# A nine-way router: "not computed" as a choice of its own, one summing instruction per tile for the slots

## The chip, the cores and the metric

The kernel runs on one core of a Trainium2 chip. The metric is the device time of one execution in microseconds; the time given is the median of the timed runs. Views of the trace come from one further, profiled execution. The engines are PE (TensorE: matmuls, with PEld for its weight loads), DVE (VectorE), ACT (ScalarE), POOL (GpSimd) and SP (SyncE, which issues most of the DMAs).

## What is computed

Three layers follow one another: an attention with a threshold per row, a dense two-matrix layer with a smooth activation, and a mixture of eight experts. 4 batches of 576 rows give 2304 tokens of width 512. The change lies in the third layer's router:

```python
skip_score = x @ w_skip
do_compute = skip_score > 0
out = x.copy()
xc = x[do_compute]
logits = xc @ w_gate                       # 8 experts
e_idx = np.argmax(logits, axis=1)
probs = softmax(logits)
gate_w = probs[np.arange(len(xc)), e_idx]
for e in range(8):
    mask = e_idx == e
    h = np.maximum(xc[mask] @ w1[e], 0.0)
    y[mask] = gate_w[mask, None] * (h @ w2[e])
out[do_compute] = xc + y
```

## The kernel before

The attention is worked off in units of one head and 128 rows (two heads for the last 64 rows of a batch), the dense layer in ten blocks of 128 or 256 tokens. Both run interleaved, since the blocks need only the rows that are finished. A planner (`Plan`, `P.op`) gets every operation with its engine, a nominal duration, what it follows, its buffers and a due time; it simulates the engines and so fixes one order of issue per engine. The order depends on the nominal durations, not on what the operation's code contains. At run time each engine works off its queue in that order, and an instruction that waits holds up all behind it on its engine.

The router (`class Route`) takes the dense layer's blocks in eleven groups: one of a single tile of 128 tokens, seven of two tiles, three of a single tile at the end. For each group the planner issues:

- `rsq` (ACT), for the last three groups `rtp` (PE) and `rsq`: `begin` takes the small tile `sm`, which has a few columns per tile of the group, and the squares of the row are summed into `ss`.
- `rinv` (DVE, L279): `pow2_scale` (L28 to L31, four instructions) makes a power of two `inv` and its inverse `rin` for each tile.
- `rhi`, `rlo`, `rtr`, `rlog`: the rows are split into two halves of 16 bits, transposed by DMA, and multiplied with the nine columns of weights (eight experts and skip) into PSUM, `d["l"]`. The last three groups use PE for the transposition and multiply in fp32.
- `rpick` (DVE, L312 to L340): the maximum, a weight 8 to 1 for each expert that reaches it, the largest of these, and the one-hot row `c` of eight columns, multiplied with `cmp` (skip score above 0).
- `rrank` (PE, L342): a matmul with a triangle and one with ones and `csum` count, for each token, how many earlier tokens chose each expert.
- `rslot` (DVE, L351 to L361): the count plus the expert's offset, times `c`, summed: the row of the table `tbl` into which the token goes. The offset begins at -BIG, so a token that isn't computed gets a row beyond the table, which the write leaves out. Then `csum` takes in `c`.
- `rexp` (ACT, L366), `rgate` (DVE, L369 to L377): the gate, and the table entry `meta` of three numbers: token, gate times `rin`, and `inv`.
- `rsc` (POOL, L381): an indirect DMA writes the entries into `tbl`.

For the last two groups one-hot matrices (L276) are made from the slots, with which PE takes the first two experts' rows straight from the tiles. Behind the router lie the counts, the load of the table and the experts.

The constants are made at `rconst` (L206), between two pieces of the attention. The first DVE instructions there fill `ones16` and `csum`; POOL makes the triangle, the weights `w8` (L212), the offsets `offs` (L213) and the token numbers `tok`.

```python
    def rinv(s, ts):
        d = s.st[ts]
        for i in range(len(ts)):
            pow2_scale(s.nc, None, d["ss"][:, i], d["inv"][:, i], d["rin"][:, i], 195)
```

Of the kernel before, what the change touches and what calls it, by code (L numbers as in the profile page):

```python
# [188 lines left out]
class Route:  # L189
    def __init__(s, nc, cst, dram, w_skip, w_gate):  # L190
        s.nc = nc
        s.w_skip, s.w_gate = w_skip, w_gate
        s.tri = cst.tile([128, 128], F16, name="tri")
        s.ones16 = cst.tile([128, 128], F16, name="ones16")
        s.w8 = cst.tile([128, NE], F32, name="w8")
        s.offs = cst.tile([128, NE], F32, name="offs")
        s.wg = cst.tile([128, 4, NE + 1], F32, name="wg")
        s.wg16 = cst.tile([128, 2, 4, NE + 1], F16, name="wg16")
        s.wsc = cst.tile([128, 4], F32, name="wsc")
        s.csum = cst.tile([128, NE], F16, name="csum")  # L200
        s.tok = cst.tile([128, NT // 128], I32, name="tok")
        s.tbl = dram.tile([NE * NT, 3], I32, name="tbl")
        s.x2d = dram.tile([NT, DM], F32, name="x2d")
        s.st = {}

    def consts(s):  # L206
        nc = s.nc
        nc.vector.memset(s.ones16, 1.0)
        nc.vector.memset(s.csum, 0.0)
        nc.gpsimd.affine_select(out=s.tri, in_=s.ones16, pattern=[[1, 128]], compare_op=ALU.is_gt, fill=0.0, base=0,  # L210
                                channel_multiplier=-1)
        nc.gpsimd.iota(s.w8, pattern=[[-1, NE]], base=NE, channel_multiplier=0, allow_small_or_imprecise_dtypes=True)  # L212
        nc.gpsimd.iota(s.offs, pattern=[[NT, NE]], base=-BIG, channel_multiplier=0,  # L213
                       allow_small_or_imprecise_dtypes=True)
        nc.gpsimd.iota(s.tok, pattern=[[128, NT // 128]], base=0, channel_multiplier=1)
        big = s.junk.bitcast(I32)[:, 0:NT * NE // 128]
        nc.gpsimd.iota(big, pattern=[[0, NT * NE // 128]], base=BIG, channel_multiplier=0)
        nc.sync.dma_start(out=s.wg[:, :, 0:NE], in_=s.w_gate.rearrange("(k p) e -> p k e", p=128))
        nc.sync.dma_start(out=s.wg[:, :, NE:NE + 1], in_=s.w_skip.rearrange("(k p) -> p k", p=128)[:, :, None])
        for i in range(3):  # L220
            nc.sync.dma_start(out=s.tbl.rearrange("(i a b) c -> i a (b c)", i=3, a=128)[i], in_=big)
# [11 lines left out]

    def begin(s, ts, xs):
        sm = s.wk.tile([128, 114], F32, tag="sm", bufs=4, name="sm")
        v, o = {}, 0
        for k, w in (("ss", 1), ("inv", 1), ("kap", 1), ("mx", 1), ("nb", 1), ("cmp", 1), ("top", 1), ("sl", 1),
                     ("sum", 1), ("rin", 1), ("va", 8), ("vb", 8), ("vc", 8)):
# [73 lines left out]
    def pick(s, ts, plain=False):  # L312

        nc, d, n = s.nc, s.st[ts], len(ts)
        c = s.wk.tile([128, 2, NE], F16, tag="c", bufs=4, name="c")[:, 0:n]
        d["c"] = c
        l = d["l"][:, :, 0:NE]
        w8 = s.w8[:, None, :].to_broadcast([128, n, NE])

        def wide(x):  # L320
            return x.to_broadcast([128, n, NE])
        nc.vector.tensor_reduce(out=d["mx"], in_=l, axis=AX.X, op=ALU.max)
        if n == 1:
            nc.vector.scalar_tensor_tensor(out=d["va"][:, 0], in0=l[:, 0], scalar=d["mx"][:, 0], in1=s.w8, op0=ALU.is_ge, op1=ALU.mult)
        else:
            nc.vector.tensor_tensor(out=d["va"], in0=l, in1=wide(d["mx"]), op=ALU.is_ge)
            nc.vector.tensor_tensor(out=d["va"], in0=d["va"], in1=w8, op=ALU.mult)
        nc.vector.tensor_scalar(out=d["cmp"], in0=d["l"][:, :, NE:NE + 1], scalar1=0.0, scalar2=None, op0=ALU.is_gt)
        nc.vector.tensor_reduce(out=d["top"], in_=d["va"], axis=AX.X, op=ALU.max)
        if n == 1:  # L330
            nc.vector.scalar_tensor_tensor(out=c[:, 0], in0=s.w8, scalar=d["top"][:, 0], in1=d["cmp"][:, 0].to_broadcast([128, NE]),
                                           op0=ALU.is_equal, op1=ALU.mult)
        else:
            nc.vector.tensor_tensor(out=d["vb"], in0=w8, in1=wide(d["top"]), op=ALU.is_equal)
            nc.vector.tensor_tensor(out=c, in0=d["vb"], in1=wide(d["cmp"]), op=ALU.mult)
        if plain:
            nc.vector.memset(d["kap"], 1.0)
        else:
            nc.vector.tensor_scalar(out=d["kap"], in0=d["rin"], scalar1=s.wsc[:, 2:3], scalar2=None, op0=ALU.mult)
        nc.vector.scalar_tensor_tensor(out=d["nb"], in0=d["mx"], scalar=-1.0, in1=d["kap"], op0=ALU.mult, op1=ALU.mult)  # L340

    def rank(s, ts):  # L342
        d = s.st[ts]
        for i in range(len(ts)):
            r = d["r"][:, i, 0:NE]
# [22 lines left out]

    def rgate(s, ts):  # L369
        nc, d, n = s.nc, s.st[ts], len(ts)  # L370
        m = s.wk.tile([128, 2, 3], I32, tag="meta", bufs=4, name="meta")
        d["m"] = m
        nc.vector.tensor_scalar(out=d["sum"], in0=d["sum"], scalar1=1e-9, scalar2=None, op0=ALU.add)
        nc.gpsimd.tensor_copy(out=m[:, 0:n, 0], in_=s.tok[:, ts[0]:ts[0] + n])
        nc.vector.reciprocal(out=d["sum"], in_=d["sum"])
        nc.vector.tensor_copy(out=m[:, 0:n, 2:3].bitcast(F32), in_=d["inv"])
        nc.vector.tensor_tensor(out=m[:, 0:n, 1:2].bitcast(F32), in0=d["sum"], in1=d["rin"], op=ALU.mult)  # L377

    def scatter(s, ts, i):
        d = s.st[ts]  # L380
# [338 lines left out]
def body(ctx, tc, q, k, v, tau, w_in, w_out, w_skip, w_gate, w1, w2, out):  # L719
# [968 lines left out]
```

## Time and profile before

| | us |
|---|---|
| median of three timed runs | 984.99 |
| lowest and highest of them | 982.43, 986.34 |
| the profiled execution | 978.3 |
| its span, from the first to the last instruction | 976.3 |
| PE busy | 813.4 (83%) |
| DVE busy | 708.7 (73%) |
| ACT busy | 612.2 (63%) |
| POOL busy | 497.7 (51%) |

The page's slices and the table of stretches are read first: they show where each engine is busy. The lists of waits say which engine ended an idle time. The groups by line and shape give the mean duration of one instruction, which includes the time in which it was held after its start. The timeline gives single instructions in their order, with the idle time in front of each.

### The profile page before, as it was taken

The page shows a single profiled execution, that of the slowest core. Times are in us where ns is not written, and L with a number is a line of the kernel's source. Part 1 is how long each engine was busy: PE and PEld are TensorE (multiplying, and loading weights), DVE is VectorE, ACT ScalarE, POOL GpSimd, SP SyncE. Part 2 cuts the span into 40 slices and gives each one's busy share as a digit, 9 for nine tenths or more (in the row PEclk, how much of TensorE's full clock was granted, in tenths as well). Part 3 has the DMA queues.
Part 4 walks back from the last instruction along what each step waited for, and adds up shares of the span by engine and source line. Part 5 has one row for each costly group of instructions (what it writes and reads, how often), then busy time and mean ns, then how long its engine had stood idle before and what let it go on. Part 6 is the DMA issues. An engine that isn't in the chain of part 4 may idle for free. (4 is left out here: it accounts for less than half of the span.)

```text
span 976.3 us, 19887 instructions
## 1 busy us (share of the span) xinstructions
PE 813.4 (83%) x7340; PEld 588.1 (60%) x7340; DVE 708.7 (73%) x1433; ACT 612.2 (63%) x1003; POOL 497.7 (51%) x454
## 2 busy tenths in 40 slices
PE   6476875778889899857998988979989887999994
PEld 3243765666667576644676765667666546566762
DVE  4888889896978678769779788878868646434431
ACT  5173677888877788766886888877866644222110
POOL 2055447775856574736656766655734323332211
PEclk9999986889689899986999998999999998999998
DMA  9924986946946768685586694586680545887920
GB/s 251 389 76 108 254 194 125 211 86 187 219 95 126 170 150 174 163 164 120 100 169 137 124 228 113 129 170 113 143 252 23 160 174 160 234 261 208 311 95 18
DMA packets 254144, 160.63 MB, mean 165 GB/s; under 512 B 205646, under 2 KB 206030, under 8 KB 254032
## 3 DMA queue, kind: packets, MB, share of 16 engines
q1 hardware_dynamic: 245952, 145.01, 61.8%
q10 hardware_dynamic: 5184, 9.44, 2.8%
q0 software_dynamic: 2896, 4.74, 1.5%
q8 instruction: 64, 1.05, 0.5%
q14 instruction: 48, 0.39, 0.1%
HBM read 100.71 MB, written 12.57 MB: 116 GB/s over the span
## 5 line engine op out<-in xcount | busy, mean ns | idle before, releaser
L1144 PE MATMUL hp<-xt,win 128*128 128x256 f16 (+1 forms) x1920 | 212.7, 267 | 2.1 <-DVE g L795 2.1
L1201 PE MATMUL o<-wout,g 128*128 128x512 f16 x816 | 196.6, 393 | 6.7 <-DVE g L1190 2.6
L1144 PEld LDWEIGHTS <-win 128*128 128x128 f16 x1920 | 169.8, 100 | 25.1 <-issue 2.2
L1049 POOL TENSOR_TENSOR hl<-e,hl 128x512 f16<-128x512 f32 x122 | 145.5, 1193 | 0.0
L991 PE MATMUL s<-kt,qh 128*128 128x288 f32 x320 | 112.9, 368 | 31.9 <-DVE e L1037 18.0
L1201 PEld LDWEIGHTS <-g 128*128 128x128 f16 x816 | 80.0, 101 | 98.0 <-issue 12.0
L995 DVE TENSOR_REDUCE nm<-s 128x1 f32<-128x576 f32 x144 | 106.9, 751 | 37.6 <-PE s L991 37.4
L1070 PE MATMUL xps<-vt,pt 128*128 128x64 f16 (+1 forms) x2016 | 94.4, 205 | 41.6 <-DMA pt<-hl 36.2
L1070 PEld LDWEIGHTS <-pt 128*128 128x128 f16 x2016 | 82.5, 104 | 57.0 <-DMA pt<-hl 43.3
L1048 POOL TENSOR_TENSOR hl<-e,hl 128x64 f16<-128x64 f32 x122 | 51.1, 419 | 128.2 <-ACT hl L791 52.8
L1037 DVE SCALAR_TENSOR_TENSOR e<-s,th,e 128x576 f32<-128x576 f32 x128 | 101.9, 809 | 9.5 <-ACT e L1022 7.9
L1022 ACT ACTIVATE e<-s,nm 128x576 f32<-128x576 f32 x128 | 92.3, 734 | 18.2 <-DVE nm L995 17.5
L1180 POOL TENSOR_TENSOR u<-u,g 128x1024 f32<-128x1024 f32 x32 | 76.9, 2411 | 43.6 <-ACT u L1176 43.4
L991 PE MATMUL s<-kt,ql 128*128 128x288 f32 x320 | 97.0, 318 | 0.0
L991 PEld LDWEIGHTS s<-kt,qh 128*128 128x128 f32 x320 | 67.3, 210 | 42.5 <-issue 31.3
L791 ACT ACTIVATE hl<-e 128x576 f16<-128x576 f32 x97 | 65.2, 678 | 34.6 <-DVE e L1037 20.9
L590 PE MATMUL o<-w,ht 128*128 128x512 f32 x176 | 77.8, 597 | 2.2 <-PEq L645 1.3
L991 PEld LDWEIGHTS s<-kt,ql 128*128 128x128 f32 x320 | 68.1, 213 | 0.7
L570 PEld LDWEIGHTS <-w1q 128*128 128x128 f16 x1056 | 61.8, 100 | 8.6 <-issue 6.4
L590 PEld LDWEIGHTS o<-w,ht 128*128 128x128 f32 x176 | 32.6, 190 | 39.9 <-issue 38.3
L422 ACT ACTIVATE ws<-ws 128x512 f32<-128x512 f32 x64 | 39.9, 623 | 21.3 <-DMA ws<-in_w_dram 20.1
L570 PE MATMUL g<-xt,w1q 128*128 128x128 f16 x864 | 50.4, 219 | 2.3 <-POOL w1q L484 1.5
(230 smaller groups left out, 1482.6 us busy)
## 6 DMA issues: line engine op xcount, KB each, us to landing
ws<-in_w_dram SPq DMA_DIRECT2D x64, 256.0 KB, 3.4
stage<-in_w_dram SPq DMA_DIRECT2D x16, 1024.0 KB, 7.4
w<-in_w_dram SPq DMA_DIRECT2D x16, 1024.0 KB, 9.3
qst<-in_q_dram SPq DMA_DIRECT2D x38, 256.0 KB, 4.4
vst<-in_v_dram SPq DMA_DIRECT2D x35, 256.0 KB, 4.5
win<-in_moe_w_in_dram SPq DMA_DIRECT2D x16, 512.0 KB, 7.7
w<-in_moe_w_out_dram SPq DMA_DIRECT2D x16, 512.0 KB, 4.9
kst<-in_k_dram SPq DMA_DIRECT2D x24, 288.0 KB, 4.2
```

The costliest lines, as they stand in the source:

```text
L570: s.nc.tensor.matmul(out=p[:, f], lhsT=w[:, c, a, k, f * 128:(f + 1) * 128], rhs=xt[:, 4 * b + k], start=m == 0, stop=m == 11)
L590: s.nc.tensor.matmul(out=o, lhsT=ht[:, k], rhs=w[:, k // 4, k % 4, :], start=k == 0, stop=k == 7)
L791: nc.scalar.activation(out=out, in_=in_, func=AF.Copy, scale=scale)
L991: nc.tensor.matmul(out=o, lhsT=x, rhs=y, start=start and n == 0, stop=n == len(ops) - 1)
L995: nc.vector.tensor_reduce(out=nm, in_=sp[i][:, :, 0:HS], axis=AX.XY, op=ALU.max, negate=True)
L1022: nc.scalar.activation(out=e, in_=sp[i][:, :, 0:HS], func=AF.Exp, bias=nmx[i])
L1037: nc.vector.scalar_tensor_tensor(out=ep[i], in0=sp.pop(i)[:, :, 0:HS], scalar=thr.pop(i), in1=ep[i], op0=ALU.is_ge, op1=ALU.mult, accum_ou ...
L1049: ENG[eng].tensor_tensor(out=t[:, S + 64:2 * S], in0=e[:, 0:512], in1=t[:, 0:512], op=ALU.subtract)
L1070: nc.tensor.matmul(out=o, lhsT=p[:, blk, :], rhs=vv[:, a, h0:h0 + w], start=(n == 0), stop=(n == len(seq) - 1))
L1144: nc.tensor.matmul(out=hp[j, p][:, i * TB:(i + 1) * TB], lhsT=win[wa][:, kk, f * 128:(f + 1) * 128], rhs=xt[j][:, xa, kk, 0:TB], start=(n ...
L1180: ENG[eng].tensor_tensor(out=u, in0=u, in1=gt[j, r], op=ALU.mult)
L1201: nc.tensor.matmul(out=o, lhsT=g[:, ga, i * TB + s * 128:i * TB + (s + 1) * 128], rhs=wout[f // 8][:, f % 8, wa, :], start=(f == 0 and n = ...
```

## The change

`inv` moves into the table entry `meta`, which `begin` now takes; POOL's copy of the token numbers moves there too, from `rgate`, and `rgate` no longer copies `inv`. `rinv` works on both tiles of a group at once. "Not computed" is a ninth column with weight 9, so the largest weight decides between it and the experts, and `c` and `csum` have nine columns. The offsets are added on PE, by one more matmul per tile; the sum over the product with `c` is one instruction per tile that writes its accumulator. Factors that were products of two tensors become instructions with one number per partition, one per tile. The constants for this are made with short memsets on DVE. The plan's nominal durations are unchanged.

```diff
-        s.w8 = cst.tile([128, NE], F32, name="w8")
-        s.offs = cst.tile([128, NE], F32, name="offs")
+        s.w9 = cst.tile([128, NE + 1], F32, name="w9")
+        s.offs = cst.tile([128, NE + 1], F16, name="offs")
-        s.csum = cst.tile([128, NE], F16, name="csum")
+        s.csum = cst.tile([128, NE + 1], F16, name="csum")
...
-        nc.gpsimd.iota(s.w8, pattern=[[-1, NE]], base=NE, channel_multiplier=0, allow_small_or_imprecise_dtypes=True)
-        nc.gpsimd.iota(s.offs, pattern=[[NT, NE]], base=-BIG, channel_multiplier=0,
-                       allow_small_or_imprecise_dtypes=True)
+        nc.gpsimd.iota(s.w9, pattern=[[-1, NE + 1]], base=NE, channel_multiplier=0, allow_small_or_imprecise_dtypes=True)
+        nc.vector.memset(s.w9[:, NE:NE + 1], NE + 1.0)
+        nc.vector.memset(s.offs, 0.0)
+        for e in range(NE + 1):
+            nc.vector.memset(s.offs[0:1, e:e + 1], float(e * NT))
...
     def begin(s, ts, xs):
         sm = s.wk.tile([128, 114], F32, tag="sm", bufs=4, name="sm")
+        m = s.wk.tile([128, 2, 3], I32, tag="meta", bufs=4, name="meta")
+        s.nc.gpsimd.tensor_copy(out=m[:, 0:len(ts), 0], in_=s.tok[:, ts[0]:ts[0] + len(ts)])
...
-        s.st[ts] = dict(v, x=xs)
+        s.st[ts] = dict(v, x=xs, m=m, inv=m[:, 0:len(ts), 2:3].bitcast(F32))
...
     def rinv(s, ts):
         d = s.st[ts]
-        for i in range(len(ts)):
-            pow2_scale(s.nc, None, d["ss"][:, i], d["inv"][:, i], d["rin"][:, i], 195)
+        pow2_scale(s.nc, None, d["ss"], d["inv"], d["rin"], 195)
...
     def pick(s, ts, plain=False):
-        nc.vector.tensor_reduce(out=d["mx"], in_=l, axis=AX.X, op=ALU.max)
-        if n == 1:
-            nc.vector.scalar_tensor_tensor(out=d["va"][:, 0], in0=l[:, 0], scalar=d["mx"][:, 0], in1=s.w8, op0=ALU.is_ge, op1=ALU.mult)
-        else:
-            nc.vector.tensor_tensor(out=d["va"], in0=l, in1=wide(d["mx"]), op=ALU.is_ge)
-            nc.vector.tensor_tensor(out=d["va"], in0=d["va"], in1=w8, op=ALU.mult)
-        nc.vector.tensor_scalar(out=d["cmp"], in0=d["l"][:, :, NE:NE + 1], scalar1=0.0, scalar2=None, op0=ALU.is_gt)
+        nc.vector.tensor_reduce(out=d["mx"], in_=d["l"][:, :, 0:NE], axis=AX.X, op=ALU.max)
+        nc.vector.tensor_scalar(out=d["va"][:, :, NE:NE + 1], in0=d["l"][:, :, NE:NE + 1], scalar1=0.0, scalar2=NE + 1.0, op0=ALU.is_le, op1=ALU.mult)
+        for i in range(n):
+            nc.vector.scalar_tensor_tensor(out=d["va"][:, i, 0:NE], in0=d["l"][:, i, 0:NE], scalar=d["mx"][:, i], in1=s.w9[:, 0:NE],
+                                           op0=ALU.is_ge, op1=ALU.mult)
         nc.vector.tensor_reduce(out=d["top"], in_=d["va"], axis=AX.X, op=ALU.max)
-        if n == 1:
-            nc.vector.scalar_tensor_tensor(out=c[:, 0], in0=s.w8, scalar=d["top"][:, 0], in1=d["cmp"][:, 0].to_broadcast([128, NE]),
-                                           op0=ALU.is_equal, op1=ALU.mult)
-        else:
-            nc.vector.tensor_tensor(out=d["vb"], in0=w8, in1=wide(d["top"]), op=ALU.is_equal)
-            nc.vector.tensor_tensor(out=c, in0=d["vb"], in1=wide(d["cmp"]), op=ALU.mult)
+        for i in range(n):
+            nc.vector.tensor_scalar(out=c[:, i], in0=s.w9, scalar1=d["top"][:, i], scalar2=None, op0=ALU.is_equal)
         if plain:
             nc.vector.memset(d["kap"], 1.0)
+            nc.vector.tensor_scalar(out=d["nb"], in0=d["mx"], scalar1=-1.0, scalar2=None, op0=ALU.mult)
         else:
             nc.vector.tensor_scalar(out=d["kap"], in0=d["rin"], scalar1=s.wsc[:, 2:3], scalar2=None, op0=ALU.mult)
-        nc.vector.scalar_tensor_tensor(out=d["nb"], in0=d["mx"], scalar=-1.0, in1=d["kap"], op0=ALU.mult, op1=ALU.mult)
+            for i in range(n):
+                nc.vector.tensor_scalar(out=d["nb"][:, i], in0=d["mx"][:, i], scalar1=d["kap"][:, i], scalar2=-1.0, op0=ALU.mult, op1=ALU.mult)

     def rank(s, ts):
...
+            s.nc.tensor.matmul(out=r, lhsT=s.ones16, rhs=s.offs, start=False, stop=False)
             s.nc.tensor.matmul(out=r, lhsT=s.ones16, rhs=s.csum, start=False, stop=True)

     def slot(s, ts):
-        nc.vector.tensor_tensor(out=d["va"], in0=d["r"][:, :, 0:NE], in1=s.offs[:, None, :].to_broadcast([128, n, NE]),
-                                op=ALU.add)
-        nc.vector.tensor_tensor(out=d["va"], in0=d["va"], in1=d["c"], op=ALU.mult)
-        nc.vector.tensor_reduce(out=d["sl"], in_=d["va"], axis=AX.X, op=ALU.add)
-        nc.vector.tensor_scalar(out=si, in0=d["sl"], scalar1=float(BIG), scalar2=None, op0=ALU.add)
+        for i in range(n):
+            nc.vector.scalar_tensor_tensor(out=d["va"][:, i], in0=d["r"][:, i, 0:NE + 1], scalar=0.0, in1=d["c"][:, i], op0=ALU.add,
+                                           op1=ALU.mult, accum_out=d["sl"][:, i])
+        nc.vector.tensor_copy(out=si, in_=d["sl"])

     def rgate(s, ts):
-        m = s.wk.tile([128, 2, 3], I32, tag="meta", bufs=4, name="meta")
-        d["m"] = m
         nc.vector.tensor_scalar(out=d["sum"], in0=d["sum"], scalar1=1e-9, scalar2=None, op0=ALU.add)
-        nc.gpsimd.tensor_copy(out=m[:, 0:n, 0], in_=s.tok[:, ts[0]:ts[0] + n])
         nc.vector.reciprocal(out=d["sum"], in_=d["sum"])
-        nc.vector.tensor_copy(out=m[:, 0:n, 2:3].bitcast(F32), in_=d["inv"])
-        nc.vector.tensor_tensor(out=m[:, 0:n, 1:2].bitcast(F32), in0=d["sum"], in1=d["rin"], op=ALU.mult)
+        for i in range(n):
+            nc.vector.tensor_scalar(out=d["m"][:, i, 1:2].bitcast(F32), in0=d["sum"][:, i], scalar1=d["rin"][:, i], scalar2=None, op0=ALU.mult)
```

The row of numbers from which the last one-hot matrices are made (`jrow`) begins at 0 instead of -BIG, and the counts read the first eight columns of `csum`.

## Rows read from the trace of the kernel before

**Rows 1.** Stretch 160 to 790: busy us (instructions) per engine, clock, DMA share, GB/s

```profile
160.00:790.00 630.00, 540.73 (x5084) 403.64 (x5085) 503.67 (x1035) 489.23 (x790) 382.30 (x341) 0.92 0.67 150
```

**Rows 2.** What PE waited for, 160 to 790: us in total, times, longest

```profile
PE xps L1070 <- DMA pt<-hl: 33.2, 21, 6.4
PE s L991 <- DVE e L1037: 13.7, 8, 5.1
...
PE s L991 <- DVE sm L355: 0.2, 1, 0.2
```

**Rows 3.** DVE's groups by shape, 160 to 790: busy us, mean ns, idle before

```profile
L1037 DVE DVE_READ_ACCUMULATOR e<-s,th,e 128x1 f32 x119 | 9.5, 80 | 0.0
L327 DVE TENSOR_TENSOR sm<-sm,w 128x16 f32<-128x16 f32 x7 | 6.2, 879 | 0.2
...
L377 DVE TENSOR_TENSOR meta<-sm 128x2 f32<-128x2 f32 x7 | 3.2, 463 | 0.0
L334 DVE TENSOR_TENSOR sm<-w,sm 128x16 f32<-128x16 f32 x7 | 3.1, 444 | 0.2
L357 DVE TENSOR_TENSOR sm<-sm,c 128x16 f32<-128x16 f32 x7 | 3.0, 426 | 0.2
L376 DVE COPY meta<-sm 128x2 f32<-128x2 f32 x7 | 2.8, 404 | 0.0
...
L28 DVE TENSOR_SCALAR sm<-sm 128x1 f32<-128x1 f32 x16 | 2.3, 143 | 3.3 <-ACT rh L248 3.3
L373 DVE TENSOR_SCALAR sm<-sm 128x2 f32<-128x2 f32 x7 | 2.1, 302 | 0.9 <-ACT sm L366 0.9
L359 DVE TENSOR_SCALAR si<-sm 128x2 int32<-128x2 f32 x7 | 2.0, 283 | 0.2
...
L326 DVE TENSOR_TENSOR sm<-rps,sm 128x16 f32<-128x16 f32 x7 | 1.2, 174 | 0.2
...
L324 DVE SCALAR_TENSOR_TENSOR sm<-rps,sm,w 128x8 f32<-128x8 f32 x1 | 0.2, 225 | 0.0
```

**Rows 4.** Timeline of DVE, 361 to 367.2: start us, duration us, instruction

```profile
366.01 0.14 DVE L28 TENSOR_SCALAR sm<-sm 128x1 f32<-128x1 f32 x1
...
366.63 0.20 DVE L1001 TENSOR_SCALAR th<-nm,ntau 128x1 f32<-128x1 f32 x1
```

**Rows 5.** Timeline of DVE, 776.5 to 781.3, a two-tile group

```profile
776.81 0.18 DVE L322 TENSOR_REDUCE sm<-rps 128x2 f32<-128x16 f32 x1 [1.10 <-PE rps L308]
...
778.31 0.69 DVE L1169 TENSOR_SCALAR u<-u 128x1024 f32<-128x1024 f32 x1
779.67 0.17 DVE L355 TENSOR_TENSOR sm<-rps,offs 128x16 f32<-128x16 f32 x1 [0.67 <-PE rps L349]
...
780.29 0.17 DVE L359 TENSOR_SCALAR si<-sm 128x2 int32<-128x2 f32 x1
...
780.64 0.16 DVE L373 TENSOR_SCALAR sm<-sm 128x2 f32<-128x2 f32 x1
...
780.91 0.15 DVE L376 COPY meta<-sm 128x2 f32<-128x2 f32 x1
781.03 0.16 DVE L377 TENSOR_TENSOR meta<-sm 128x2 f32<-128x2 f32 x1
```

**Rows 6.** Timeline of DVE, 812 to 816.8, the last tile

```profile
814.72 0.16 DVE L355 TENSOR_TENSOR sm<-rps,offs 128x8 f32<-128x8 f32 x1
...
815.69 0.48 DVE L276 TENSOR_SCALAR oh<-jrow,sm 128x128 f16<-128x128 f32 x2
```

**Rows 7.** Timeline of all engines, 158 to 172, the constants

```profile
162.51 0.06 DVE L209 MEMSET csum<- 128x4 uint32 x1
...
162.64 0.29 POOL L210 TENSOR_SCALAR_AFFINE_SELECT tri<-ones 128x128 f16<-128x128 f16 x1 [0.97 <-ACT wt L791]
...
162.89 0.13 POOL L212 IOTA w<- 128x8 f32 x1
```

**Rows 8.** PE's groups by shape, 160 to 822: busy us, mean ns, idle before

```profile
L349 PE MATMUL rps<-csum,ones 128*128 128x8 f16 x18 | 2.4, 166 | 0.0
```

More of the change, by code (lines that the diff above doesn't have):

```diff
@@ L235, in begin @@
         sm = s.wk.tile([128, 114], F32, tag="sm", bufs=4, name="sm")
+        m = s.wk.tile([128, 2, 3], I32, tag="meta", bufs=4, name="meta")
+        s.nc.gpsimd.tensor_copy(out=m[:, 0:len(ts), 0], in_=s.tok[:, ts[0]:ts[0] + len(ts)])
         v, o = {}, 0
-        for k, w in (("ss", 1), ("inv", 1), ("kap", 1), ("mx", 1), ("nb", 1), ("cmp", 1), ("top", 1), ("sl", 1),
-                     ("sum", 1), ("rin", 1), ("va", 8), ("vb", 8), ("vc", 8)):
+        for k, w in (("ss", 1), ("kap", 1), ("mx", 1), ("nb", 1), ("top", 1), ("sl", 1),
+                     ("sum", 1), ("rin", 1), ("va", 9), ("vc", 8)):
             v[k] = sm[:, o:o + 2 * w].rearrange("p (s e) -> p s e", s=2)[:, 0:len(ts)]
             o += 2 * w
-        s.st[ts] = dict(v, x=xs)
+        s.st[ts] = dict(v, x=xs, m=m, inv=m[:, 0:len(ts), 2:3].bitcast(F32))
     def rsq(s, ts, xs):
@@ L314, in pick @@
         nc, d, n = s.nc, s.st[ts], len(ts)
[L315 to L321, printed above, removed]
-        nc.vector.tensor_reduce(out=d["mx"], in_=l, axis=AX.X, op=ALU.max)
-        if n == 1:
-            nc.vector.scalar_tensor_tensor(out=d["va"][:, 0], in0=l[:, 0], scalar=d["mx"][:, 0], in1=s.w8, op0=ALU.is_ge, op1=ALU.mult)
-        else:
-            nc.vector.tensor_tensor(out=d["va"], in0=l, in1=wide(d["mx"]), op=ALU.is_ge)
-            nc.vector.tensor_tensor(out=d["va"], in0=d["va"], in1=w8, op=ALU.mult)
@@ L328, in pick @@
-        nc.vector.tensor_scalar(out=d["cmp"], in0=d["l"][:, :, NE:NE + 1], scalar1=0.0, scalar2=None, op0=ALU.is_gt)
-        nc.vector.tensor_reduce(out=d["top"], in_=d["va"], axis=AX.X, op=ALU.max)
-        if n == 1:
-            nc.vector.scalar_tensor_tensor(out=c[:, 0], in0=s.w8, scalar=d["top"][:, 0], in1=d["cmp"][:, 0].to_broadcast([128, NE]),
-                                           op0=ALU.is_equal, op1=ALU.mult)
-        else:
-            nc.vector.tensor_tensor(out=d["vb"], in0=w8, in1=wide(d["top"]), op=ALU.is_equal)
-            nc.vector.tensor_tensor(out=c, in0=d["vb"], in1=wide(d["cmp"]), op=ALU.mult)
+        c = d["c"] = s.wk.tile([128, 2, NE + 1], F16, tag="c", bufs=4, name="c")[:, 0:n]
@@ L344, in rank @@
         for i in range(len(ts)):
-            r = d["r"][:, i, 0:NE]
+            r = d["r"][:, i, 0:NE + 1]
             s.nc.tensor.matmul(out=r, lhsT=s.tri, rhs=d["c"][:, i], start=True, stop=False)
@@ L352, in slot @@
         nc, d, n = s.nc, s.st[ts], len(ts)
-        si = s.wk.tile([128, 2, 1], I32, tag="si", bufs=4, name="si")[:, 0:n]
-        d["si"] = si
-        nc.vector.tensor_tensor(out=d["va"], in0=d["r"][:, :, 0:NE], in1=s.offs[:, None, :].to_broadcast([128, n, NE]),
-                                op=ALU.add)
-        nc.vector.tensor_tensor(out=d["va"], in0=d["va"], in1=d["c"], op=ALU.mult)
-        nc.vector.tensor_reduce(out=d["sl"], in_=d["va"], axis=AX.X, op=ALU.add)
-        nc.vector.tensor_scalar(out=si, in0=d["sl"], scalar1=float(BIG), scalar2=None, op0=ALU.add)
+        si = d["si"] = s.wk.tile([128, 2, 1], I32, tag="si", bufs=4, name="si")[:, 0:n]
+        for i in range(n):
+            nc.vector.scalar_tensor_tensor(out=d["va"][:, i], in0=d["r"][:, i, 0:NE + 1], scalar=0.0, in1=d["c"][:, i], op0=ALU.add,
+                                           op1=ALU.mult, accum_out=d["sl"][:, i])
+        nc.vector.tensor_copy(out=si, in_=d["sl"])
         for i in range(n):
@@ L386, in counts @@
         p = ps[:, 0, 0:NE]
-        nc.tensor.matmul(out=p, lhsT=s.ones16, rhs=s.csum, start=True, stop=True)
+        nc.tensor.matmul(out=p, lhsT=s.ones16, rhs=s.csum[:, 0:NE], start=True, stop=True)
         nc.vector.tensor_reduce(out=cm, in_=p, axis=AX.X, op=ALU.max)
@@ L1429, in slots @@
         R.jrow = M.wa.tile([128, 128], F32, tag="jrow", bufs=1, name="jrow")
-        nc.gpsimd.iota(R.jrow, pattern=[[1, 128]], base=-BIG, channel_multiplier=0, allow_small_or_imprecise_dtypes=True)
+        nc.gpsimd.iota(R.jrow, pattern=[[1, 128]], base=0, channel_multiplier=0, allow_small_or_imprecise_dtypes=True)
     P.op("slots", "POOL", 150, slots, 900, ["att_end"])
```

## The prediction

> **What bounds the kernel now.** The first view is busy time by stretch. The work that the change touches lies between 160 us, where the router's constants are made, and 817 us, where the last table entries are written. From 160 to 790 us no engine is full: PE is busy 540.7 of 630 us, DVE 503.7, ACT 489.2 and POOL 382.3 [rows 1]. So PE stands idle 89.3 us there, and a shorter DVE instruction counts only where PE, or something that PE needs, waits for it. The second view, what PE waited for in the same stretch, sizes that. The longest entry is the transposed weights that come back by DMA, 33.2 us; eleven entries name DVE as the engine that ended the wait, from 13.7 us down to 0.2 us, 44.0 us in all [rows 2]. 44.0 of 89.3 is 0.49. I use 0.49 as the share of a DVE change that reaches the end of the kernel. It is an estimate: the DMA waits also hang on DVE through the softmax pieces, which speaks for more; DVE's own 126 us of idle time in the stretch (630 less 503.7) speaks for less.
>
> The third view is DVE's groups by shape. What matters there is the distance between a short instruction's mean and its time when nothing holds it. A product of two 16-wide tensors in SBUF takes 879 ns in the mean at L327, while the same size with one operand in PSUM takes 174 ns at L326 [rows 3]. The seven executions of L327 thus hold 4.9 us of standing still; by the same subtraction L334 holds 1.9 and L357 1.8. The two-wide L376, L377, L373 and L359 take 404, 463, 302 and 283 ns in the mean, against 0.15 to 0.17 us where they run free [rows 5]: 1.8, 2.1, 1.0 and 0.8 us more over seven each. The one-wide L28 is never held: 143 ns over sixteen [rows 3]. POOL works 382.3 us of the stretch [rows 1]. So the change has two faces, the count of instructions and which of them can be held.
>
> **rinv.** Two-tile groups (seven of them) go from eight DVE instructions to four. One tile's four take 366.01 to 366.63, 0.62 us [rows 4]: 7 x 0.62 = 4.3 us less. But the four that stay become two-wide. The two-wide tensor_scalars nearest to them, L373 and L359, were held 1.8 us in 14 executions, 0.125 us each; 28 such instructions cost 3.5 us. Bounds: never held, 0; or the first of each four held as L327 (0.70 us) and the others as L334 (0.27 us), 7 x 1.51 = 10.6 us. I take 3.5, since width and kind are those of L373 and L359. Net -0.8 us, from -4.3 to +6.3. The chain now starts only when both squares are done; the second tile's half did so before, and the result is no later.
>
> The row shows one-wide instructions never held and two-wide ones held at times. The Trainium skill, "SBUF — State Buffer", section "Who interferes with whom", says that a DVE instruction with two SBUF inputs, or a copy, cast or tensor_scalar in a two-port mode, shares a port pair with GpSimd and blocks until the other is done, while one SBUF input outside these modes never does. Its page "VectorE: DVE Perf Modes", section "What auto-detection actually checks", lets a two-port mode in where the outermost extents are even or equal. By that rule rinv's new form can be held, the old one could not, and the nine-wide compare below can be held too; the trace agrees on L28, L326 and L327, and shows no nine-wide case. Without the rule rinv's 3.5 us could be left out, and the sum would be 1.7 us lower; with it they stay.
>
> **pick.** Two-tile groups go from nine instructions to ten. The old chain takes 776.81 to 778.31, 1.50 us [rows 5]; one more link, but two of the products become one fused instruction per tile that reads PSUM (225 ns at L324 [rows 3]). I take 0, with 0.5 us over seven groups on either side. The held ones: L327 and L334 go, and what first needs SBUF twice or a wide mode is now the compare that writes c. No row shows that form. I let its first execution inherit L327's 4.9 us and price the second at 0.125 x 7 = 0.9, in place of L334's 1.9: -1.0 us, from -6.8 (neither is held) to 0.
>
> **slot and rgate.** slot goes from add, product, reduction and conversion to one summing instruction per tile and a conversion. The old form takes 779.67 to 780.64, 0.97 us [rows 5]. The new one is 2 x (0.225 + 0.08 for the accumulator's read [rows 3]) plus two csum additions and the conversion, about 0.96 by durations: 0, from -1.4 to +0.7 over the stage. L357's 1.8 us of being held moves on to the conversion or vanishes; I take half, -0.9, from -2.6 (L359's goes too) to 0. rgate loses the copy of inv, 0.12 us from start to start [rows 5], in the eight groups of the stretch, and gains a second product, which I price the same, in seven of them: -0.1 us. L376 and L377 were held 3.9 us; the new one-wide products look like L28. What they waited for may pass to the next big instruction, so half: -1.9, from -3.9 to 0.
>
> **Constants.** One POOL iota goes, eleven short DVE memsets come, 0.06 us each by L209: 0.7 us. One writes a column of the tile that POOL's iota fills, so DVE now waits for POOL. POOL was itself waiting there (0.97 us idle before L210), ran L210 at 162.64 and the iota from 162.89 to 163.02, when DVE had been done at 162.57 [rows 7]: 0.45 us and a hand-over. Behind it on DVE stands a mask of the attention, and the transposes and PV products after it. I take +1.4 us, from +0.7 to twice that.
>
> **Costed at nothing.** rank has one more matmul per tile, 18 of 166 ns, issued back to back with their like [rows 8], up to 3.0 us of PE if nothing overlapped; PE's idle 89.3 us hide it, and the last one is in the tail below. POOL's copy of the token numbers moves from the gate to the start of a group, so it passes whatever POOL queues between; only the table write reads it, and it needs its buffer free from four groups before. The ninth column adds one element to each row. No queue of SP changes.
>
> **The tail.** The last tile's slot decides when the one-hot matrices, and with them the last transposition, can start: L355 at 814.72 to L276 at 815.69, 0.97 us [rows 6]. The new chain is 0.225 + 0.08 + conversion and csum, some 0.5: -0.45 us, directly on the path.
>
> **The sum.** In the stage -0.8 - 1.0 + 0 - 0.9 - 0.1 - 1.9 + 1.4 = -3.3 us of DVE. Times 0.49 that is -1.6; with the tail -2.1 us. The profiled span of 976.3 us becomes 974.2, its execution of 978.3 us 976.2. The three timed runs lie higher (median 984.99); I put the difference on the median: **982.9 us**. The ends of the terms, each times 0.49 and with the tail: -4.3 - 0.5 - 6.8 - 1.4 - 2.6 - 0.1 - 3.9 + 0.7 = -18.9, that is -9.7 us, 975.3; and +6.3 + 0.5 + 0 + 0.7 + 0 - 0.1 + 0 + 2.8 = +10.2, that is +4.5 us, 989.5.
>
> **Rivals.** *What was held vanishes* (faster): the standing still at L327, L334, L357, L376 and L377, 12.5 us, is in no new instruction and rinv is never held. DVE gets 4.3 + 12.5 + 0.1 - 1.4 = 15.5 us less: -7.6 - 0.45 us, **976.9**. For it: the new products read PSUM or are one-wide, like L326 and L28. Against it: csum's additions, the conversion and the compare still stand in the same place, and POOL's instruction has to end some time.
>
> *rinv is held* (slower): 28 two-wide instructions in a chain, where after each POOL can take its next piece, are each held as L327, 0.70 us. DVE gets -4.3 + 19.7 - 0.1 + 1.4 = +16.7 us: +8.2 - 0.45, **992.7**. It is slower by more than 0.5% from 0.50 us each, since 0.49 x (28 x 0.50 - 3.0) - 0.45 = 4.9. Against it: L373 and L359 show 0.125.
>
> *Hidden* (no change): DVE's idle time takes up all that the stage gains, and only the tail is left: **984.5**.
>
> **How the numbers follow.** Forecast 0.40, vanishes 0.30, hidden 0.13, rinv held 0.14; 0.03 for something slower that I don't see. About 0.5% (4.9 us, so below 980.1 or above 989.9) is what a measurement of this kernel can tell from no change. The forecast's own span crosses 980.1, so 0.06 of its 0.40 counts as faster. Faster 0.36, same 0.47, slower 0.17. The range takes in the ends of the terms: 975 to 990.
>
> **What would show it.** In the trace of the changed kernel: L28's successors two-wide, seven chains of four, with a mean between 0.16 us (never held) and 0.3 (as priced), or 0.8 (the slower rival); the compare that writes c with a mean near 0.9 in its first execution; the rgate products at 0.15; a DVE wait for POOL of about half a microsecond near 163 us; DVE's busy time between 160 and 790 us lower by some 4 us, PE's waits lower by half of that; the last tile's slot about 0.5 us long. It is wrong if DVE's time falls by 10 us and the end moves with it, if the two-wide chains stand still, or if PE's clock takes another course between the two traces.

## The result and the profile after

The changed kernel takes 976.14 us (median of 20 runs, 968.86 to 985.42); the kernel before, beside it, 985.02 us (20 runs, 976.58 to 989.21). The ratio is 0.9912 [0.9888, 0.9935]: by the ratio 8.7 us faster, with 6.4 and 11.0 as the ends. The forecast was 982.9 us, 2.1 us faster. The direction and the range held, the size did not. A ratio leaves out executions more than 1.5% above the fastest of their kernel, so it can differ a little from the quotient of two medians. The profiled execution of the changed kernel took 973.97 us, its span is 971.9.

The page of the changed kernel, engines' busy time:

```profile
span 971.9 us, 19916 instructions
PE 815.9 (84%) x7358; PEld 591.3 (61%) x7358; DVE 698.5 (72%) x1422; ACT 612.7 (63%) x1003; POOL 499.3 (51%) x453
```

DVE is 10.2 us less busy than the 708.7 of before, with only eleven instructions fewer. In the stretch of [rows 1], in the same columns:

```profile
160.00:790.00 630.00, 549.04 (x5131) 408.89 (x5131) 498.69 (x1048) 491.01 (x793) 383.81 (x341) 0.93 0.66 150
```

DVE falls from 503.67 to 498.69, 5.0 us, where some 4 were foreseen. PE's idle time falls from 89.3 to 81.0 us, but 47 more matmuls lie in the stretch (5131 after 5084), so this is no gain by itself. What PE waited for in that stretch (us in total, times, longest), to be held against [rows 2]:

```profile
PE xps L1059 <- DMA pt<-hl: 26.1, 16, 5.2
PE s L980 <- DVE e L1026: 16.4, 9, 5.1
...
PE s L980 <- DVE sm L349: 0.2, 1, 0.2
```

The eleven entries that name DVE sum to 44.3 us, as 44.0 did before. What became shorter in this pair of profiles is the wait for the transposed weights by DMA, 33.2 to 26.1 us; a second profile of the kernel before, shown below, has 23.8 there, so this is scatter between executions. PE's waits for DVE did not fall by half of DVE's gain; they did not fall.

DVE's groups by shape, 160 to 790 (busy us, mean ns, idle before), the lines that answer to [rows 3]:

```profile
L1158 DVE TENSOR_SCALAR u<-u 128x1024 f32<-128x1024 f32 x36 | 33.1, 920 | 1.9 <-ACT u L1154 1.9
...
L1037 DVE TENSOR_TENSOR hl<-e,hl 128x64 f16<-128x64 f32 x22 | 22.3, 1016 | 0.8 <-ACT hl L780 0.8
...
L326 DVE TENSOR_SCALAR c<-w,sm 128x9 f16<-128x9 f32 x16 | 8.1, 546 | 0.3
...
L351 DVE CAST si<-sm 128x2 int32<-128x2 f32 x7 | 3.4, 491 | 0.2
L29 DVE TENSOR_SCALAR meta<-meta 128x2 int32<-128x2 int32 x7 | 3.0, 430 | 0.2
L322 DVE SCALAR_TENSOR_TENSOR sm<-rps,sm,w 128x8 f32<-128x8 f32 x16 | 3.0, 223 | 0.0
...
L366 DVE TENSOR_SCALAR meta<-sm 128x1 f32<-128x1 f32 x16 | 2.8, 210 | 0.3
...
L28 DVE TENSOR_SCALAR meta<-sm 128x2 f32<-128x2 f32 x7 | 2.5, 350 | 4.2 <-ACT rh L252 4.2
...
L31 DVE TENSOR_SCALAR sm<-meta 128x2 int32<-128x2 int32 x7 | 2.1, 300 | 0.2
L349 DVE SCALAR_TENSOR_TENSOR sm<-rps,c 128x9 f32<-128x9 f32 x16 | 2.1, 163 | 5.5 <-PE rps L343 4.8 <-ACT sm L358 0.7
...
L30 DVE TENSOR_SCALAR meta<-meta 128x2 int32<-128x2 int32 x7 | 1.2, 177 | 0.2
```

The standing still has moved. L327 is gone, and the compare that writes `c` (L326) now takes 546 ns in the mean where it takes 240 free (the last tile, below): 16 x 0.306 = 4.9 us, what L327 held. It is spread over both executions of a two-tile group: the seven first ones take 0.62 us in the mean (0.9 was foreseen) and the seven second ones 0.56. The four two-wide scales L28 to L31 take 8.8 us in 28 executions, 0.314 each against 0.165 free. What reads PSUM (L322, L349) is never held: its longest executions take 0.23 and 0.17 us. One chain of scales shows what being held looks like (timeline of DVE; start, duration, instruction):

```profile
365.87 0.27 DVE L28 TENSOR_SCALAR meta<-sm 128x2 f32<-128x2 f32 x1
366.17 1.08 DVE L29 TENSOR_SCALAR meta<-meta 128x2 int32<-128x2 int32 x1
367.29 0.17 DVE L30 TENSOR_SCALAR meta<-meta 128x2 int32<-128x2 int32 x1
367.49 0.17 DVE L31 TENSOR_SCALAR sm<-meta 128x2 int32<-128x2 int32 x1
```

It is the group of [rows 4]. POOL in the same stretch (timeline of POOL):

```profile
364.94 1.17 POOL L1037 TENSOR_TENSOR hl<-e,hl 128x64 f16<-128x64 f32 x1
366.07 1.16 POOL L1038 TENSOR_TENSOR hl<-e,hl 128x512 f16<-128x512 f32 x1
```

L28 and L29 each end 0.03 us after an instruction of POOL that was running when they started (366.11 and 367.23), and L30 and L31, with POOL idle, run free. This holds throughout: in the two profiles of the kernel before and the three of the changed one that this document goes by, 99 of the router's small DVE instructions between 160 and 822 us take over 0.06 us more than the shortest of their kind, and every one of them ends 0.02 to 0.04 us behind the end of a POOL instruction. The old one-wide scales of this group, from 365.39 to 366.72 in the kernel before, kept to 0.14 to 0.16 us while POOL ran there:

```profile
365.59 1.15 POOL L1049 TENSOR_TENSOR hl<-e,hl 128x512 f16<-128x512 f32 x1
```

So being held is a lump that lasts until POOL is done, and not a tax on each link; whether a chain meets one depends on what POOL runs just then. Of the seven two-wide chains here, four run free (0.77 to 0.78 us, POOL idle throughout), two lose one lump and one, at 628.82, loses two. In the other two profiles of the changed kernel five run free. In the group shown the new four cost more than the old eight, 1.79 us (365.87 to 367.66) against 1.24; over all seven groups it is 8.8 us against 8.5.

The constants and the last tile (timeline of DVE; in brackets the idle time and what ended it), which answer to [rows 6, 7]:

```profile
163.04 0.07 DVE L209 MEMSET csum<- 128x9 f16 x1
...
163.63 0.06 DVE L213 MEMSET w<- 128x1 f32 x1 [0.52 <-POOL w L212]
163.64 0.07 DVE L214 MEMSET offs<- 128x9 f16 x1
163.76 0.12 DVE L216 MEMSET offs<- 1x1 f16 x8
163.85 0.82 DVE L1026 SCALAR_TENSOR_TENSOR e<-s,th,e 128x576 f32<-128x576 f32 x1
...
807.14 0.24 DVE L326 TENSOR_SCALAR c<-w,sm 128x9 f16<-128x9 f32 x1
...
808.17 0.17 DVE L349 SCALAR_TENSOR_TENSOR sm<-rps,c 128x9 f32<-128x9 f32 x1
808.26 0.08 DVE L349 DVE_READ_ACCUMULATOR sm<-rps,c 128x1 f32 x1
808.38 0.15 DVE L351 CAST si<-sm 128x1 int32<-128x1 f32 x1
808.45 0.16 DVE L353 TENSOR_TENSOR csum<-csum,c 128x9 f16<-128x9 f16 x1
808.52 0.48 DVE L280 TENSOR_SCALAR oh<-jrow,sm 128x128 f16<-128x128 f32 x2
```

DVE waits 0.52 us for POOL, and the mask stands 0.74 us behind the end of L209 (163.11 to 163.85). The last slot takes 0.35 us (808.17 to 808.52), not 0.97. It starts 6.55 us earlier than in [rows 6], while the span is only 4.4 us shorter: in this pair of executions about 2 us were lost again behind the router.

### The profile page after: what moved, and what is told of

It reads as the page before. It is cut to its first block, busy times and chain, and to the rows that moved or that the text cites. A ratio compares the mean times of both kernels' runs of the same rounds, so it can differ in the third digit from the quotient of the medians.

```text
span 971.9 us, 19916 instructions
## 1 busy us (share of the span) xinstructions
PE 815.9 (84%) x7358; PEld 591.3 (61%) x7358; DVE 698.5 (72%) x1422; ACT 612.7 (63%) x1003; POOL 499.3 (51%) x453
## 5 line engine op out<-in xcount | busy, mean ns | idle before, releaser
L1133 PE MATMUL hp<-xt,win 128*128 128x256 f16 (+1 forms) x1920 | 215.5, 269 | 1.4 <-DVE g L784 1.4
L1038 POOL TENSOR_TENSOR hl<-e,hl 128x512 f16<-128x512 f32 x122 | 147.6, 1210 | 0.0
L984 DVE TENSOR_REDUCE nm<-s 128x1 f32<-128x576 f32 x144 | 106.9, 751 | 44.3 <-PE s L980 44.0
L1037 POOL TENSOR_TENSOR hl<-e,hl 128x64 f16<-128x64 f32 x122 | 49.2, 404 | 126.8 <-ACT hl L780 53.0
L1169 POOL TENSOR_TENSOR u<-u,g 128x1024 f32<-128x1024 f32 x32 | 77.0, 2413 | 40.6 <-ACT u L1165 40.5
L952 POOL TENSOR_TENSOR ql<-qst,qh 128x512 fp32r<-128x512 f32 x30 | 39.5, 1318 | 25.2 <-ACT qh L780 17.2
```

The lines of the kernel that those rows point to most:

```text
L984: nc.vector.tensor_reduce(out=nm, in_=sp[i][:, :, 0:HS], axis=AX.XY, op=ALU.max, negate=True)
L1038: ENG[eng].tensor_tensor(out=t[:, S + 64:2 * S], in0=e[:, 0:512], in1=t[:, 0:512], op=ALU.subtract)
L1133: nc.tensor.matmul(out=hp[j, p][:, i * TB:(i + 1) * TB], lhsT=win[wa][:, kk, f * 128:(f + 1) * 128], rhs=xt[j][:, xa, kk, 0:TB], start=(n ...
L1169: ENG[eng].tensor_tensor(out=u, in0=u, in1=gt[j, r], op=ALU.mult)
```

## The experiments

Two questions stood open. Where do the 8.7 us come from: one part of the change, the parts together, or a larger share of DVE's time at the end than 0.49? And how far can a difference of this size be trusted? The first eight kernels ran on one chip, the last four on another; the comparison on record names none. Each was timed against the kernel before on its own chip. The changed kernel itself was not run on the second chip.

### The same two kernels again

The changed kernel was run twice more, without an edit.

> The changed kernel once more, beside the parts that follow. Theory A (the prediction's: a DVE microsecond counts 0.49 at the end, what is held mostly moves on) gives -2.1 us. Theory B (each DVE microsecond of the router counts in full or more, because others stand in line behind it) gives about what was measured, -7 to -10 us. Theory C (one part alone does it, by a wait that goes) gives the same total, but the parts alone would then be one at -6 or more and the others near 0.

> The changed kernel a third time, since its ratio to before was 0.9912 [0.9888, 0.9935] the first time and 0.9972 [0.9939, 1.0005] the second. Theory A (a DVE microsecond of the stage counts 0.49): 0.998, about 2 us less. Theory B (counts in full or more): 0.991 to 0.993. The mean of the three is what the later comparisons go by.

Measured: 973.30 us (12 runs), ratio 0.9972 [0.9939, 1.0005]; and 974.39 us (12 runs), 0.9972 [0.9944, 1.0]. That is 2.7 us faster, twice, not 8.7. The changed kernel takes what it took on record (976.14). It is the kernel before that differs: 976.29 us (35 runs) and 976.13 us (34 runs) here, 985.02 on record.

So the kernel before was run as if it were a change, on the other chip, with no edit.

> The kernel before itself, on the chip of the other runs, for its trace there and for how far two samples of one kernel lie apart. Both theories: ratio 1, within 0.35%. If the chip, and not the kernel, makes the difference between 985 us (record) and 976 us (here), the trace here is some 9 us shorter somewhere, and the place tells what the change could win there that it can't win here.

Measured: 988.18 us (12 runs) against 985.37 (17 runs), ratio 1.0043 [1.0009, 1.0076]. One kernel against itself comes out 0.4% slower, with an interval that leaves out 1. So an interval here can miss by about that much. The kernel before takes 985 us or more on this chip, as on record. Its page, engines' busy time:

```profile
PE 824.5 (84%) x7340; PEld 594.7 (61%) x7340; DVE 711.4 (72%) x1433; ACT 611.6 (62%) x1003; POOL 501.0 (51%) x454
```

Its longest wait of PE between 160 and 790 us, to be held against the 33.2 us of [rows 2] and the changed kernel's 26.1:

```profile
PE xps L1070 <- DMA pt<-hl: 23.8, 17, 3.7
```

Two of its DVE groups by shape (columns as above; L1169 and L1048 are L1158 and L1037 of the changed kernel):

```profile
L1169 DVE TENSOR_SCALAR u<-u 128x1024 f32<-128x1024 f32 x36 | 34.4, 955 | 1.9 <-ACT u L1165 1.9
L1048 DVE TENSOR_TENSOR hl<-e,hl 128x64 f16<-128x64 f32 x22 | 27.7, 1260 | 1.9 <-ACT hl L791 0.9 <-POOL hl L1049 0.9
```

L1048's code is the same in both kernels. Its mean is 1260 ns here and 1132 in the profile of before on record, and 1016, 1131 and 1112 in the three profiles of the changed kernel: it scatters between executions. Five profiles of the unaltered pair of kernels are now there, two of before and three of the changed. DVE's page busy is 708.7 and 711.4 against 698.5, 700.9 and 697.8 us: 11 us less in the mean.

### One part alone

Three kernels are the kernel before with one part of the change, and two the changed kernel less one part.

Scales of both tiles at once, alone (first chip), and the changed kernel with scales per tile again (second chip):

```diff
-        for i in range(len(ts)):
-            pow2_scale(s.nc, None, d["ss"][:, i], d["inv"][:, i], d["rin"][:, i], 195)
+        pow2_scale(s.nc, None, d["ss"], d["inv"], d["rin"], 195)
```

> The kernel before, with the scales of both tiles at once and nothing else changed: 28 DVE instructions less. Theory A: -0.4 us (4.3 us less by count, 3.5 us more held, times 0.49). Theory B: -3 to -4.5 us. Theory C: 0 or -6 and more.

> The changed kernel with the scales computed per tile again, one-wide: 28 DVE instructions more, 4.3 us, and none of them held, 4.1 us less by the trace of the changed kernel. Theory A with its bounds: level, within 1 us. Theory B (the count decides): 2 to 4 us slower.

Measured: alone 977.09 us, ratio 1.0003 [0.9967, 1.0038]. The changed kernel without it (the edit above reversed) 972.94 us, 0.9862 [0.9819, 0.9905] against the 985.37 of its chip. The scales alone do nothing that can be measured. Against the changed kernel of the record (0.9912) the one without them is no slower either, so no gain of the scales shows. Their groups, of the kernel with scales alone (its profiled execution, 984.86 us, is the longest of its twelve; of the old ones L28 is in [rows 3]):

```profile
L29 DVE TENSOR_SCALAR sm<-sm 128x2 int32<-128x2 int32 x7 | 3.0, 431 | 0.2
L31 DVE TENSOR_SCALAR sm<-sm 128x2 int32<-128x2 int32 x7 | 2.1, 301 | 0.2
L28 DVE TENSOR_SCALAR sm<-sm 128x2 f32<-128x2 f32 x7 | 1.4, 193 | 3.9 <-ACT rh L248 3.9
L30 DVE TENSOR_SCALAR sm<-sm 128x2 int32<-128x2 int32 x7 | 1.2, 177 | 0.2
```

7.7 us in 28 executions where 56 one-wide ones took 56 x 0.151 = 8.5: halving the count gains 0.8 us of DVE.

The ninth choice alone (`w9`, the new pick, nine columns of `c` and `csum`; the slots still with an addition, a product and a sum):

```diff
+        nc.vector.tensor_scalar(out=d["va"][:, :, NE:NE + 1], in0=d["l"][:, :, NE:NE + 1], scalar1=0.0, scalar2=NE + 1.0, op0=ALU.is_le, op1=ALU.mult)
...
+        for i in range(n):
+            nc.vector.tensor_scalar(out=c[:, i], in0=s.w9, scalar1=d["top"][:, i], scalar2=None, op0=ALU.is_equal)
```

> The kernel before, with the ninth column and the new selection, but the old slot computation (offsets added on DVE from a nine-wide tile), the old gate and the scales per tile. Theory A: -0.2 us (1.0 us less held, 0.6 us more at the constants). Theory B: -1 to -2 us. Theory C: 0 or -6 and more.

Measured: 971.07 us, 0.9962 [0.9931, 0.9993].

`inv` in the table entry and a product per tile for the gate, alone:

```diff
-        nc.vector.tensor_copy(out=m[:, 0:n, 2:3].bitcast(F32), in_=d["inv"])
-        nc.vector.tensor_tensor(out=m[:, 0:n, 1:2].bitcast(F32), in0=d["sum"], in1=d["rin"], op=ALU.mult)
+        for i in range(n):
+            nc.vector.tensor_scalar(out=d["m"][:, i, 1:2].bitcast(F32), in0=d["sum"][:, i], scalar1=d["rin"][:, i], scalar2=None, op0=ALU.mult)
```

> The kernel before, with inv inside the table entry, the token numbers copied by POOL at the start of a group, and the gate's product with one number per partition, one per tile. Theory A: -1.0 us (2.0 us of DVE, most of it held, times 0.49). Theory B: -2 us. Theory C, if POOL's copy between the gate's instructions is the wait that goes: -6 and more.

Measured: 972.93 us, 0.9970 [0.9936, 1.0003].

The changed kernel with the old slots (offsets on DVE, no matmul for them, no summing instruction, none of the short memsets for `offs`):

```diff
-        for i in range(n):
-            nc.vector.scalar_tensor_tensor(out=d["va"][:, i], in0=d["r"][:, i, 0:NE + 1], scalar=0.0, in1=d["c"][:, i], op0=ALU.add,
-                                           op1=ALU.mult, accum_out=d["sl"][:, i])
-        nc.vector.tensor_copy(out=si, in_=d["sl"])
+        nc.vector.tensor_tensor(out=d["va"], in0=d["r"][:, :, 0:NE + 1], in1=s.offs[:, None, :].to_broadcast([128, n, NE + 1]),
+                                op=ALU.add)
+        nc.vector.tensor_tensor(out=d["va"], in0=d["va"], in1=d["c"], op=ALU.mult)
+        nc.vector.tensor_reduce(out=d["sl"], in_=d["va"], axis=AX.X, op=ALU.add)
+        nc.vector.tensor_scalar(out=si, in0=d["sl"], scalar1=float(BIG), scalar2=None, op0=ALU.add)
```

> The changed kernel with the old slot computation (offsets added on DVE, product, reduction, conversion) and without the offset matmul: scales, ninth column and table entry changed, the slots not. Theory A: 1 us slower than the changed kernel (0.45 of the tail, half of the 0.9 held). Theory B: 1 to 2 us slower. If the parts add up as the single ones did (0, -4 and -3 us by their medians), it is level with the changed kernel or faster by 2 to 4 us.

Measured: 973.45 us, 0.9965 [0.9939, 0.9991]. On this chip the ninth choice alone gives 0.38%, the gate alone 0.30%, everything but the slots 0.35%, and the whole 0.28%. The gains do not add up, and with the 0.4% of the kernel against itself none can be told from another, and hardly from nothing. On this chip the whole gives 2.7 us, so there are no 8.7 us here that one part could carry; the parts were not run on the second chip, apart from the scales. The slots' summing instruction shows no gain of its own.

### What a microsecond of DVE costs at the end

To measure the share, DVE work was added to the changed kernel: dependent one-wide tensor_scalars on a spare column, which nothing else reads, in each of the seven two-tile groups. Such an instruction is never held and takes 0.187 us from start to start. First 16 of them, behind the scales or behind the gate's products:

```diff
         pow2_scale(s.nc, None, d["ss"], d["inv"], d["rin"], 195)
+        if len(ts) == 2:
+            t = d["sm"][:, 100:101]
+            s.nc.vector.tensor_scalar(out=t, in0=d["ss"][:, 0], scalar1=2.0, scalar2=None, op0=ALU.mult)
+            for i in range(16 - 1):
+                s.nc.vector.tensor_scalar(out=t, in0=t, scalar1=0.5, scalar2=None, op0=ALU.mult)
```

> The changed kernel with sixteen one-wide DVE instructions, each waiting for the one before, put behind the scales in each of the seven two-tile groups: 16 x 0.19 x 7 = 21 us more of DVE, none of which POOL can hold. Theory A: +10 us against the changed kernel. Theory B: +21 us or more. Hidden (DVE's idle time takes it up, as the kernel with the scales alone suggests, which was level with before): 0 to +3 us.

> The same sixteen instructions, but behind the gate's products at the end of each group, where the table write alone waits for the router. Theory A and theory B give the same as for the place behind the scales, since DVE works in order and all behind it is late alike. If the place counts (what the instructions stand in front of), the two differ by more than 4 us.

Measured: 980.28 us, 1.0027 [0.9998, 1.0056], and 978.99 us, 1.0030 [1.0001, 1.0058]. Against the changed kernel of the same chip (974.39) that is 5.9 and 4.6 us for 7 x 16 x 0.187 = 21 us of DVE: 0.25. No difference between the places shows. Each ratio is uncertain by 0.3%, 3 us; with 5.2 plus or minus 3 us the share lies between about 0.1 and 0.4.

Then 48 of them behind the scales (`16 - 1` becomes `48 - 1`), and 48 that are two elements wide (`t` is `[:, 100:102]` as two columns and the first reads all of `ss`), on the second chip.

> The changed kernel with 48 instead of sixteen one-wide DVE instructions behind the scales of each two-tile group: 48 x 0.19 x 7 = 64 us more of DVE. By the share of 0.26 that the sixteen gave: +17 us against the changed kernel. By the prediction's 0.49: +31 us. If the idle time of DVE is used up on the way (some 130 us between 160 and 790), the share grows: +25 us or more.

> The same 48 instructions, but two elements wide, which POOL can hold by the rows of the changed kernel (the four of the scales were held 0.15 us each in the mean). If each is held alike: 336 x 0.15 = 50 us more of DVE than the one-wide form, +13 us at a share of 0.26. If only the first of a chain meets a POOL instruction, since POOL then stands behind DVE: 7 x 0.5 = 4 us more, +1 us.

Measured: 1023.75 us, 1.0386 [1.0346, 1.0426], and 1035.89 us, 1.0523 [1.0482, 1.0564]. Against the nearest relative of the changed kernel on that chip, the one with scales per tile (972.94), the one-wide chain costs 50.8 us for 7 x 48 x 0.187 = 63 us: 0.81, by the intervals of the two ratios between about 0.7 and 0.9. What PE waited for between 160 and 790 us with the one-wide chain of 48:

```profile
PE s L985 <- DVE th L995: 21.2, 6, 7.8
...
PE xtp L1092 <- DVE x L1079: 17.9, 6, 12.1
```

the last of these lines with the chain of 16 behind the scales:

```profile
PE xtp L1092 <- DVE x L1079: 11.8, 6, 6.4
```

and DVE's group of the added instructions, 160 to 830 us, in the one-wide chain of 48, then in the two-wide:

```profile
L291 DVE TENSOR_SCALAR sm<-sm 128x1 f32<-128x1 f32 x329 | 50.6, 154 | 11.4
```

```profile
L291 DVE TENSOR_SCALAR sm<-sm 128x2 f32<-128x2 f32 x329 | 65.8, 200 | 11.2
```

With lumps of 9 us PE stands up to 12.1 us at a time for DVE's x, with lumps of 3 us up to 6.4. A microsecond of DVE has no one price: 0.25 in lumps of 3 us, 0.81 in lumps of 9.

The two chains ran on different chips, and 48 instructions also add three times as much in all, so it could be the chip or the sum in place of the lump. The traces speak against the sum, and in part against the chip. The start of the n-th instruction of ACT (1003 in each kernel) in a trace with the chains, less its start in a trace without them, tells how late the kernel is by then. From just before a chain to 10 us behind its end, this grows by 9 us at the first chain of 48, which is 9.0 us long, and by 48 to 49 us at all seven, whichever of four traces without chains is taken: the three of the changed kernel, or that of its relative on the second chip. At the first chain of 16 behind the scales, 3.0 us long, it grows by about 2 us, at all seven, in either place, by 7 to 9 of 21. The later chains of 48 cost no more than the first (6 to 9 us, the last 3), so the price does not rise with what was added before. On both chips the loss is made at the chains; that a chain of 16 costs as little on the second chip was not tried.

The two-wide chain takes 46 ns more per instruction, 15.2 us in 329; the end moves by 12.1. Of the 46 ns, 16 are the longer free duration (170 against 154 ns). The other 30 sit in seven of the 329 instructions, which take 1.07 to 2.28 us; the rest run free.

## Why the prediction was right or wrong

**rinv.** Right in size. -4.3 by count and +3.5 held gave -0.8 us of DVE; the kernel with the scales alone shows -0.8. Held time per instruction was taken as 0.125 us; it is 0.11 there (7.7 us in 28, less 0.165 free), 0.15 in the first profile of the changed kernel and 0.11 in the other two. The mean hides how it comes about: two or three of seven chains lose one or two lumps of 1.1 to 1.3 us, the others nothing. The slower rival wanted 0.70 on each of 28. That the Trainium skill ("SBUF — State Buffer", "Who interferes with whom") has two-port tensor_scalars block where others do not, agrees with all of these rows: 329 one-wide instructions at 154 ns, the two-wide groups at means of up to 431, those that read PSUM at 163 and 223.

**The held instructions.** Partly right. The compare that writes `c` holds 4.9 us, as much as L327 did, where 5.8 were priced, and the conversion L351 takes 491 ns where L357 and the old conversion took 426 and 283. The rival in which it vanishes named nearly the number of the record (976.9), but not the mechanism. The time by which the router's small instructions between 300 and 790 us stand over their shortest execution sums to 17.7 and 19.6 us before, and to 16.5, 18.0 and 16.2 after: 1.7 less in the mean, where the terms of the sum give 0.3. It is not a fixed sum that is handed round, though. The kernel with the scales alone has 23.3, and the changed kernel with scales per tile 13.9: each lump belongs to an instruction that met one of POOL's.

**The parts in DVE time.** The durations of the router's instructions, summed by part from single instructions (mean of the two profiles of before, then of the three of the changed kernel):

| part | before | changed | difference | foreseen |
|---|---|---|---|---|
| rinv | 10.9 | 10.5 | -0.4 | -0.8 |
| pick | 24.5 | 25.1 | +0.6 | -1.0 |
| slot, with the last tile's | 16.7 | 13.8 | -2.9 | -1.35 |
| rgate | 10.6 | 9.0 | -1.6 | -2.0 |
| constants, without the wait | 0.2 | 0.9 | +0.7 | +0.7 |
| sum | 62.9 | 59.3 | -3.6 | -4.45 |

The sum of the steps held to within a microsecond. Its parts are less sure: pick gained nothing and slot twice the price, but the two profiles of before lie up to 2.3 us apart in a part, by where the lumps fell. The gate's products take 210 ns, as L1001, one-wide with a number per partition, does in [rows 4], and not the 150 of L28. The constants cost the mask 0.74 us, 0.52 of it waiting for POOL; 1.4 was taken, since the short memsets were counted end to end, and eight of them take 0.12 us together. The tail is -0.62 us where -0.45 was priced.

**DVE as a whole.** Missed. The page's busy time falls by 11 us in the mean of the profiles; in the stretch it is 7.0 (503.7 and 507.6 before, 498.7, 499.5 and 497.8 after), where some 4 were foreseen. Of the 11 the router's own instructions give 3.6; all other DVE instructions, whose code the change leaves alone, take 713.6 to 714.2 us in the three profiles of the changed kernel, and 717.9 and 719.7 in the two of before, 5.0 less in the mean; the remaining 2.4 is more overlap of one instruction with the next. The term missing from the sum is what the neighbours gain. That the shorter router causes it is not shown: the kernels with part of the change lie between and above, at 714.6 to 717.5, one profile each, and with the one-wide chains of 48, where the router is 52 us longer, the others take 703.7 us, less than in either kernel.

**The share.** Mis-sized. 0.49 came from the names in the list of waits [rows 2]. That list says 44 us of DVE before and 44.3 after, with DVE's time 5 us shorter: it is no derivative of the end with respect to DVE. Measured by added work, the share is 0.25 in small lumps (0.1 to 0.4); that work taken away counts like work added is assumed. On the first chip the errors of the two terms would cancel: 11 x 0.25 + 0.62 = 3.4 us, beside 2.7 measured and 2.1 foreseen. With 3 us of uncertainty on the 2.7, that the forecast came so close there is luck as much as working.

**What stays open: the record's 8.7 us.** Where the kernel before takes 976 us the change gives 2.7; where it takes 985 or more, 8.7 (the record) and 12.4 (the changed kernel with scales per tile, 972.94 against 985.37). The changed kernel and this relative take 973 to 976 us each time. So the difference sits in the kernel before, on some chips or occasions; two chips don't tell which. The prediction's own condition for being wrong, "DVE's time falls by 10 us and the end moves with it", came true on record: 10.2 us of DVE between the two pages, 8.7 at the end. On the first chip the end did not move so. The range held the record, but by luck: its lower end of 975.3 was made mainly for held time that vanishes, and that did not vanish. PE's clock took no other course (0.932 before, 0.934 after over the span on record) and does not explain the difference: the kernel before was granted 0.924 in the mean on the second chip and 0.926 and 0.929 on the first, where it is 9 us faster. Among 220 executions, each taken against the mean of its own kernel and group, without those with chains of 48, 0.01 of clock goes with 1.3 us. No trace of the kernel before was taken on the first chip, so where in the kernel the 9 us lie can't be read. Profiles of both kernels side by side on both chips, several of each, would be the next step; that was not tried.

## What to carry to other kernels

Price an edit by its own instructions; that part of the sum came out within a microsecond. For what is held, look at what POOL runs at the same moment, and not at a mean over all executions. Don't take the share that reaches the end from who is named in a list of waits: add a known amount of work at the place in question, in lumps of the size that is at stake, and read the price from the end. Below one per cent, run the kernel before against itself, and on a second chip, before a cause is looked for.

## What the runs showed of the hardware

A small DVE instruction that POOL holds ends 0.02 to 0.04 us behind POOL's instruction, in all 99 cases of five profiles: L29 took 1.08 us at 366.17, and 0.17 where POOL was idle. One-wide scales took 0.14 to 0.16 us with POOL busy or idle. In two-wide chains of four, two or three of seven met such a lump; in chains of 48, seven of 329 instructions did. Eight one-element memsets take 0.12 us together. And one kernel, unaltered, takes 976 us on one chip and 985 to 988 on another, while its successor takes 973 to 976, and a near relative of that 973 on the slower chip.
